# Matmul widths chosen on the chip by an expert's token count, and rows turned between its two products

## The chip, the cores and the metric

The kernel runs on one core of a Trainium2 chip. A core has five engines with instruction streams of their own: TensorE (PE, matrix products and transposes), VectorE (DVE), ScalarE (ACT), GpSimd (POOL) and SyncE (SP, which here only issues DMAs). Each engine's sequencer takes the instructions in order and hands them to the engine. The metric is the device time of one execution in microseconds; the time of a version is the median over its runs.

## The reference

Two stages. The first is attention over a short window with some global positions, for 4 batches of 768 positions and 8 heads of 64 numbers. Its result, 3072 rows (tokens) of 512 numbers, is the input of the second, a mixture of eight experts, of which each token uses one:

```python
xn = x / (norm(x) + 1e-6);  en = expert_emb / (norm(expert_emb) + 1e-6)
logits = xn @ en.T / tau
expert_idx = argmax(logits, axis=1)
gate_w = softmax(logits)[arange(N), expert_idx]
for e in range(8):
    mask = expert_idx == e
    h = maximum(x[mask] @ w1[e], 0)          # 512 -> 1024
    out[mask] = gate_w[mask, None] * (h @ w2[e])   # 1024 -> 512
```

All numbers are float32. How many tokens an expert gets is known only while the kernel runs.

## The kernel before, in words

The attention stage (`window_attention`) writes the 3072 rows to `x_dram` and routes them: for each token it finds the expert, its rank among the expert's tokens and its gate, and scatters the pair (token number, gate) to a slot of the table `meta`. Expert e owns the slots from e*3072 on, filled in order of rank; unused slots hold token number 3072 (a row of zeros in `x_dram`, and out of bounds for `out`) and gate 0. The tile `cnt` holds the tokens counted for each expert.

The expert stage is a loop over eight experts with a fixed capacity of 512 slots (`CAP`), that is four tiles of 128. The function `load_rows` loads the slots (`emt`), makes the token numbers whole numbers (`ids`, line 636) and gathers the rows by four indirect DMAs (`xg`, line 640). The function `expert` then does, in this order:

- 16 transposes on PE (line 655), four to a bank of PSUM, each bank copied by DVE into `xT` (line 656), which has the 512 slots along its free dimension;
- the first product: eight blocks of 128 hidden numbers, two to a tile `big` (two banks), each block over four pieces of 128 inputs, always 512 slots wide (line 664); ACT applies the Relu to both blocks at once (line 666). In float32 the profile shows two matmul instructions for each `matmul` of the code, so a first product has 64;
- the second product: for each of the four tiles of slots, eight pieces of hidden numbers into one bank `work` (line 671); DVE scales by the gate into `y` (line 674) and POOL scatters the rows to `out` (line 675). Again 64 matmul instructions.

Four `work` banks and two `big` tiles fill the eight banks of PSUM. The weights of an expert, 2 MB each for `w1` and `w2`, lie in one of two buffers, and SP loads the next ones when the buffer comes free. A scheduler sets the order of all engines' instructions and the semaphores between them.

After the last expert, `leftover` handles what the fast path can't: experts with more than 512 tokens. A flag is loaded into a register of every engine (line 699), and a branch (line 700) skips the pass when nothing is left.

Of the kernel before, what the change touches and what calls it, by code (L numbers as in the profile page):

```python
# [9 lines left out]
F32 = mybir.dt.float32  # L10
I32 = mybir.dt.int32
AF = mybir.ActivationFunctionType
ALU = mybir.AluOpType
AX = mybir.AxisListType
PSUM = bass.MemoryType.PSUM

P = 128
NEG = 1e9
CAP = 512

# [47 lines left out]
def empty_slots(k):  # L70

    k.nc.sync.dma_start(k.meta[:].rearrange("(p c) w -> p c w", p=P), k.fill[:])
# [57 lines left out]
def load_weights(k, e, w):  # L130
    nc = k.nc
    nc.sync.dma_start(w[0][:], k.w1[e].rearrange("(c p) f -> p c f", p=P))
    nc.sync.dma_start(w[1][:], k.w2[e].rearrange("(f p) m -> p f m", p=P))


def new_weights(k, pool):
    w1 = pool.tile([P, k.NC, k.F], F32, name="w1t", tag="w1t")
    w2 = pool.tile([P, k.NF, k.DM], F32, name="w2t", tag="w2t")
    return w1, w2
# [137 lines left out]
def window_attention(k, ctx):  # L277
    nc, tc, NT, D, B, S, H, E = k.nc, k.tc, k.NT, k.D, k.B, k.S, k.H, k.E

    def pool(name, bufs, **kw):  # L280
        return ctx.enter_context(tc.tile_pool(name=name, bufs=bufs, **kw))

    sp_p, od_p, tp_p = (pool("wa_sp", 1, space=PSUM), pool("wa_od", 4, space=PSUM),
                        pool("wa_tp", 2, space=PSUM))
    const = pool("wa_const", 1)
# [340 lines left out]
def load_rows(k, slots):  # L626

    nc, NJ = k.nc, CAP // P
    mt = k.gp.tile([P, NJ, 2], F32, name="emt", tag="emt")
    i = nc.sync.dma_start(mt[:], slots.rearrange("(p j) w -> p j w", p=P))  # L630
    for sc in k.scatters or []:
        k.tc.add_manual_dep(i.ins, sc.name,
                            mybir.DependencyInfo(mybir.DependencyClass.Sync, mybir.DependencyReason.DATA),
                            reason="a slot comes from any of the scatters")
    ids = k.gp.tile([P, NJ], I32, name="ids", tag="ids")
    nc.vector.tensor_copy(out=ids[:], in_=mt[:, :, 0])
    xgs = []
    for j in range(NJ):
        xg = k.xgp.tile([P, k.DM], F32, name="xg", tag="xg")
        nc.gpsimd.indirect_dma_start(  # L640
            out=xg[:], out_offset=None, in_=k.x_dram[:],
            in_offset=bass.IndirectOffsetOnAxis(ap=ids[:, j : j + 1], axis=0),
        )
        xgs.append(xg)
    return mt, ids, xgs


def expert(k, rows, w1, w2):
    nc, NJ = k.nc, CAP // P
    mt, ids, xgs = rows  # L650
    xT = k.xtp.tile([P, k.NC, CAP], F32, name="xT", tag="xT")
    for j in range(NJ):
        ps = k.work.tile([P, k.NC, P], F32, name="work", tag="work")
        for c in range(k.NC):
            nc.tensor.transpose(ps[:, c, :], xgs[j][:, c * P : (c + 1) * P], k.ident[:])  # L655
        nc.vector.tensor_copy(out=xT[:, :, j * P : (j + 1) * P], in_=ps[:])  # L656

    hT = k.hp.tile([P, k.NF, CAP], F32, name="hT", tag="hT")
    for f2 in range(k.NF // 2):
        ps = k.big.tile([P, 2, CAP], F32, name="big", tag="big")  # L660
        for i in range(2):
            f = 2 * f2 + i
            for c in range(k.NC):
                nc.tensor.matmul(ps[:, i, :], lhsT=w1[:, c, f * P : (f + 1) * P], rhs=xT[:, c, :],  # L664
                                 start=c == 0, stop=c == k.NC - 1)
        nc.scalar.activation(hT[:, 2 * f2 : 2 * f2 + 2, :], ps[:], AF.Relu)  # L666

    for j in range(NJ):
        ps = k.work.tile([P, k.DM], F32, name="work", tag="work")
        for f in range(k.NF):  # L670
            nc.tensor.matmul(ps[:], lhsT=hT[:, f, j * P : (j + 1) * P], rhs=w2[:, f, :],  # L671
                             start=f == 0, stop=f == k.NF - 1)
        y = k.yp.tile([P, k.DM], F32, name="y", tag="y")
        nc.vector.tensor_scalar_mul(y[:], ps[:], mt[:, j, 1:2])  # L674
        nc.gpsimd.indirect_dma_start(  # L675
            out=k.out[:, :], out_offset=bass.IndirectOffsetOnAxis(ap=ids[:, j : j + 1], axis=0),
            in_=y[:], in_offset=None, bounds_check=k.N - 1, oob_is_err=False,
        )


def leftover(k):


    nc, tc, E = k.nc, k.tc, k.E
    passes = -(-k.N // CAP)
    more = passes - 1
    flags = k.const.tile([P, 2], F32, name="flags")
    ps = k.work.tile([P, 512], F32, name="work", tag="work")
    nc.vector.tensor_tensor(out=k.good[:], in0=k.good[:], in1=k.fits[:], op=ALU.mult)
    nc.tensor.matmul(ps[:, 0:1], lhsT=k.ones[:], rhs=k.good[:], start=True, stop=True)  # L690
    nc.vector.tensor_scalar(out=flags[:, 0:1], in0=ps[:, 0:1], scalar1=float(P), scalar2=None,
                            op0=ALU.is_lt)
    most = k.const.tile([P, 1], F32, name="most")
    nc.vector.tensor_reduce(out=most[:], in_=k.cnt[:], op=ALU.max, axis=AX.X)
    nc.vector.tensor_scalar(out=flags[:, 1:2], in0=most[:], scalar1=float(CAP), scalar2=flags[:, 0:1],
                            op0=ALU.is_gt, op1=ALU.max)
    fi = k.const.tile([P, 2], I32, name="fi")
    nc.vector.tensor_copy(out=fi[:], in_=flags[:])
    any_ = nc.values_load(fi[0:1, 1:2], min_val=0, max_val=1)
    with tc.If(any_ > 0):  # L700
        redo = nc.values_load(fi[0:1, 0:1], min_val=0, max_val=1)
        with tc.If(redo > 0):
            nc.vector.memset(k.cnt[:], 0.0)
            k.scatters = None
            empty_slots(k)
            with ExitStack() as inner:
                dense_attention(k, inner)
        with ExitStack() as inner:
            expert_pools(k, inner)
            wp = inner.enter_context(tc.tile_pool(name="lo_w", bufs=1))  # L710
            rem = k.const.tile([P, E, passes], F32, name="rem")
            for j in range(passes):
                nc.vector.tensor_scalar(out=rem[:, :, j], in0=k.cnt[:], scalar1=-float(CAP * j), scalar2=0.0,
                                        op0=ALU.add, op1=ALU.max)
            nc.vector.tensor_scalar_mul(rem[:, :, 0], rem[:, :, 0], flags[:, 0:1])
            ci = k.const.tile([P, E * passes], I32, name="ci")
            nc.vector.tensor_copy(out=ci[:], in_=rem[:].rearrange("p e j -> p (e j)"))
            nc.sync.dma_start(k.c_dram[:, :], ci[0:1, :])
            with tc.For_i(0, E * passes, 1) as i:
                cv = k.gp.tile([1, 1], I32, name="cv", tag="cv")  # L720
                nc.sync.dma_start(cv[:], k.c_dram[:, bass.ds(i, 1)])
                n = nc.values_load(cv[0:1, 0:1], min_val=0, max_val=k.N)
                with tc.If(n > 0):
                    e, j = i // passes, i % passes
                    w1, w2 = new_weights(k, wp)
                    nc.sync.dma_start(w1[:], k.w1[bass.ds(e, 1)].rearrange("o (c p) f -> p (o c) f", p=P))
                    nc.sync.dma_start(w2[:], k.w2[bass.ds(e, 1)].rearrange("o (f p) m -> p (o f) m", p=P))
                    expert(k, load_rows(k, k.meta[bass.ds(e * k.N + j * CAP, CAP), :]), w1, w2)


def expert_pools(k, ctx):
# [8 lines left out]
def kernel(  # L740
# [13 lines left out]
    n = Net()  # L754
    n.tc, n.nc = tc, tc.nc
    nc = n.nc
# [19 lines left out]
    with ExitStack() as moe:  # L776
        wp_a = moe.enter_context(tc.tile_pool(name="wp_a", bufs=1))
        n.w = [new_weights(n, wp_a)]
        with ExitStack() as inner:
            window_attention(n, inner)  # L780

        n.work = ctx.enter_context(tc.tile_pool(name="work", bufs=4, space=PSUM))
        n.big = ctx.enter_context(tc.tile_pool(name="big", bufs=2, space=PSUM))
        wp_b = moe.enter_context(tc.tile_pool(name="wp_b", bufs=1))
        expert_pools(n, moe)
        for e in range(n.E):
            rows = load_rows(n, n.meta[e * n.N : e * n.N + CAP, :])
            if e > 0:
                w = new_weights(n, (wp_a, wp_b)[e % 2])
                load_weights(n, e, w)  # L790
            else:
                w = n.w[0]
            expert(n, rows, *w)
    n.scatters = None
    leftover(n)


# [26 lines left out]
```

## Time and profile before

| | |
|---|---|
| median of 3 runs | 772.12 us (770.15 to 774.82) |
| profiled execution, its own time | 777.63 us |
| its span, first to last instruction | 775.8 us |
| mean granted TensorE clock | 0.95 |
| attention, routing and first gather | until about 294 us of the span |
| eight experts | about 294 to 760 us |

In the profile, PE is TensorE's matmuls and PEld its weight loads, which run beside them. "PE big L664 x64" is a stretch of 64 matmuls of line 664 that write the tile `big`. An engine's name with a q behind it (PEldq, ACTq) is its sequencer: branches, register operations and semaphore waits that the engine itself never sees. The shape 128x512 behind a matmul is that of what streams through the array. The 40 digits of the page's slices are tenths; one slice is 19.4 us.

### The profile page before, as it was taken

The numbers are of one execution on the slowest core, as the hardware profiler recorded it, in microseconds if no ns is written. First come the engines' busy times: TensorE is split into PE (matmuls) and PEld (weight loads), VectorE is DVE, ScalarE is ACT, GpSimd is POOL, SyncE is SP. The second block draws the span as 40 slices with busy tenths as digits, with TensorE's granted clock in tenths as the row PEclk, the third lists the DMA queues.
The fourth block names the chain that finished last, engine by engine and source line by source line (L and its number), as shares of the span: only waits on it lengthen the run. The fifth ranks groups of instructions, "written<-read, shape, count | busy, mean of one in ns | idle before, by whom it ended". The sixth has DMA issues, their size and how long they took to land.

```text
span 775.8 us, 8382 instructions
## 1 busy us (share of the span) xinstructions
PE 686.5 (88%) x3394; PEld 353.0 (46%) x3394; DVE 182.4 (24%) x500; ACT 147.6 (19%) x280; POOL 112.6 (15%) x131
## 2 busy tenths in 40 slices
PE   4989986989799519999999999999999999999992
PEld 2556654555465304444444444444444444444440
DVE  2435562664366601011011011011011011011010
ACT  3545532543453200100100100100100100100100
POOL 2110022013003232012012012012012011010010
PEclk9999989898999758999999999999999999999996
DMA  9977669650110922214214115115114114000000
GB/s 185 213 129 213 177 177 39 137 118 7 37 42 16 283 48 90 83 58 174 81 53 171 78 71 175 71 64 172 64 70 168 64 77 146 0 37 14 0 26 18
DMA packets 99898, 74.57 MB, mean 96 GB/s; under 512 B 80762, under 2 KB 80890, under 8 KB 99850
## 3 DMA queue, kind: packets, MB, share of 16 engines
q1 hardware_dynamic: 90538, 58.44, 29.8%
q0 software_dynamic: 5888, 14.71, 5.4%
q10 hardware_dynamic: 3424, 0.79, 0.6%
q8 instruction: 29, 0.48, 0.3%
q14 instruction: 19, 0.16, 0.1%
HBM read 61.11 MB, written 14.90 MB: 98 GB/s over the span
## 4 chain that ended last, share of the span: by engine, by line
PE 59%; DVE 4%; DMA 3%; issue 0%; POOL 0%; SPq 0%; ACT 0%; DVEq 0%; ACTq 0%
PE big L664 29%; PE work L671 28%; DVE xT L656 2%; DMA x_dram<-xs 1%; DMA xg<-x_dram,ids 1%; DMA meta<-mt,slot 1%; DVE y L674 1%; PE tp L405 0%; PE tp L430 0%; PE tp L408 0%; DMA emt<-meta 0%; PE od L367 0%; PE work L655 0%; POOL out_dram L675 0%; SPq L630 0%
## 5 line engine op out<-in xcount | busy, mean ns | idle before, releaser
L664 PE MATMUL big<-xT,w1t 128*128 128x512 f32 x512 | 224.0, 598 | 11.2 <-DVE xT L656 11.2
L671 PE MATMUL work<-w2t,hT 128*128 128x512 f32 x512 | 221.0, 592 | 0.0
L664 PEld LDWEIGHTS big<-xT,w1t 128*128 128x128 f32 x512 | 97.4, 192 | 133.2 <-issue 120.0
L671 PEld LDWEIGHTS work<-w2t,hT 128*128 128x128 f32 x512 | 97.3, 190 | 122.5 <-issue 122.5
L674 DVE TENSOR_SCALAR y<-work,emt 128x512 f32<-128x512 f32 x32 | 24.0, 751 | 387.2 <-PE work L671 387.2
L666 ACT ACTIVATE hT<-big 128x1024 f32<-128x1024 f32 x32 | 32.8, 1023 | 432.0 <-PE big L664 432.0
L347 DVE TENSOR_TENSOR ex<-ex,table 126x384 f32<-126x384 f32 (+1 forms) x128 | 70.1, 585 | 89.0 <-ACT ex L341 89.0
L675 POOL DMA_INDIRECT out_dram<-y,ids x32 | 31.8, 995 | 337.8 <-DVE y L674 330.1
L337 PE MATMUL sp<-qT,kT 64*126 64x192 f32 (+1 forms) x512 | 66.8, 364 | 7.9 <-ACT qT L325 5.8
L367 PE MATMUL od<-ex,v 126*64 126x192 f32 (+1 forms) x576 | 62.6, 320 | 8.6 <-issue 4.6
L341 ACT ACTIVATE ex<-sp 126x768 f32<-126x768 f32 x64 | 49.1, 767 | 82.6 <-PE sp L337 60.8
L337 PEld LDWEIGHTS sp<-qT,kT 64*126 64x126 f32 x512 | 43.9, 196 | 28.1 <-issue 13.1
L367 PEld LDWEIGHTS od<-ex,v 126*64 126x64 f32 x576 | 34.1, 138 | 28.5 <-issue 18.6
L640 POOL DMA_INDIRECT xg<-x_dram,ids x32 | 30.9, 966 | 85.4 <-issue 42.9
L373 PE MATMUL od<-ex,ones 126*32 126x192 f32 (+1 forms) x576 | 36.3, 321 | 0.0
L655 PE MATMUL work<-ident,xg 128*128 128x128 f32 x128 | 17.7, 293 | 18.9 <-DMA xg<-x_dram,ids 18.9
L199 POOL DMA_INDIRECT meta<-mt,slot x24 | 23.8, 993 | 44.1 <-DVE slot L190 30.3
L655 PEld LDWEIGHTS work<-ident,xg 128*128 128x128 f32 x128 | 15.5, 151 | 23.7 <-DMA xg<-x_dram,ids 20.1
L320 PE MATMUL tp<-ident,k 128*128 128x128 f32 x96 | 19.7, 329 | 6.3 <-DMA k<-in_k_dram 6.0
L311 POOL COPY v<-v 30x1792 f32<-30x1792 f32 x8 | 13.6, 1698 | 74.8 <-DMA v<-in_v_dram 46.6
L430 PE MATMUL tp<-ident,xd 128*128 128x128 f32 x96 | 16.3, 298 | 8.2 <-DVE lh L420 6.3
L656 DVE COPY xT<-work 128x512 f32<-128x512 f32 x32 | 20.1, 682 | 6.8 <-PE work L655 6.5
(113 smaller groups left out, 297.4 us busy)
## 6 DMA issues: line engine op xcount, KB each, us to landing
w1t<-in_moe_w_dram SPq DMA_DIRECT2D x8, 2048.0 KB, 7.9
w2t<-in_moe_w_dram SPq DMA_DIRECT2D x8, 2048.0 KB, 10.8
k<-in_k_dram SPq DMA_DIRECT2D x32, 192.0 KB, 3.5
v<-in_v_dram SPq DMA_DIRECT2D x32, 192.0 KB, 4.5
x_dram<-xs SPq DMA_DIRECT2D x24, 256.0 KB, 6.3
q<-in_q_dram SPq DMA_DIRECT2D x28, 192.0 KB, 3.9
q<-in_q_dram ACTq DMA_DIRECT2D x4, 192.0 KB, 6.1
xg<-x_dram,ids POOLq DMA_INDIRECT x32
```

The source lines that it names most:

```text
L337: nc.tensor.matmul(sp[0:ROWS, e, a * n : (a + 1) * n], lhsT=t.kT[rows, j, 0:ROWS], rhs=t.qT[rows, j * BLK : j * BLK + n], start=True, stop ...
L341: nc.scalar.activation(ex, sp[0:ROWS, :, 0 : 2 * n], AF.Exp, scale=k.scale)
L347: nc.vector.tensor_tensor(out=exv, in0=exv, in1=tb, op=ALU.mult)
L367: nc.tensor.matmul(od[a][e * D : (e + 1) * D, cols], lhsT=g.v[0:ROWS, 2 * a + e, j, :], rhs=ex[:, e, a * n + c0 : a * n + c1], start=first ...
L373: nc.tensor.matmul(od[2][32 * i : 32 * i + 32, cols], lhsT=k.ones[0:ROWS, 0:32], rhs=ex[:, e, a * n + c0 : a * n + c1], start=first, stop= ...
L655: nc.tensor.transpose(ps[:, c, :], xgs[j][:, c * P : (c + 1) * P], k.ident[:])
L656: nc.vector.tensor_copy(out=xT[:, :, j * P : (j + 1) * P], in_=ps[:])
L664: nc.tensor.matmul(ps[:, i, :], lhsT=w1[:, c, f * P : (f + 1) * P], rhs=xT[:, c, :], start=c == 0, stop=c == k.NC - 1)
L666: nc.scalar.activation(hT[:, 2 * f2 : 2 * f2 + 2, :], ps[:], AF.Relu)
L671: nc.tensor.matmul(ps[:], lhsT=hT[:, f, j * P : (j + 1) * P], rhs=w2[:, f, :], start=f == 0, stop=f == k.NF - 1)
L674: nc.vector.tensor_scalar_mul(y[:], ps[:], mt[:, j, 1:2])
L675: nc.gpsimd.indirect_dma_start(out=k.out[:, :], out_offset=bass.IndirectOffsetOnAxis(ap=ids[:, j : j + 1], axis=0), in_=y[:], in_offset=No ...
```

## The change

The change does the following things.

- Slots are dealt to the tiles in order: tile j now holds the slots from 128 j on (`"(j p) w -> p j w"`), where slot 4 p + j had been in tile j. The filled slots so come first in `xT`.
- `choose_widths` compares the counts with thirteen widths, 128 and then 160 to 512 in steps of 32, on DVE, and loads two numbers for each expert into registers of PE: the index of the smallest width that holds all its tokens, and its number of tiles less one.
- The matmuls of the first product are written in thirteen versions, one for each width, for each of the four `big` tiles; those of the second in four versions, with one to four tiles. `tc.Switch` on PE picks the version (an "arm") by the register. Only PE takes part; the Relu still covers 512 columns, and all four tiles are still scaled and scattered, the unused ones to no row.
- The eight banks of PSUM are allocated once, cleared at the start, and taken in turn.
- PE's order is written out (`manual_schedule`): the rows of expert e+1 are turned between the first and the second product of expert e, and their slots and rows are fetched before expert e is computed.

```diff
+WIDTHS = [128] + list(range(160, CAP + 1, 32))
...
-    i = nc.sync.dma_start(mt[:], slots.rearrange("(p j) w -> p j w", p=P))
+    i = nc.sync.dma_start(mt[:], slots.rearrange("(j p) w -> p j w", p=P))
...
+def expert(k, rows, xT, w1, w2, choice=None, between=None):
+    nc, tc, NJ = k.nc, k.tc, CAP // P
+    mt, ids, _ = rows
+    def arms(i, n):
+        if choice is None:
+            return [n - 1]
+        return tc.Switch({PE: choice[i]}, n)
     hT = k.hp.tile([P, k.NF, CAP], F32, name="hT", tag="hT")
     for f2 in range(k.NF // 2):
-        ps = k.big.tile([P, 2, CAP], F32, name="big", tag="big")
-        for i in range(2):
-            f = 2 * f2 + i
-            for c in range(k.NC):
-                nc.tensor.matmul(ps[:, i, :], lhsT=w1[:, c, f * P : (f + 1) * P], rhs=xT[:, c, :],
-                                 start=c == 0, stop=c == k.NC - 1)
+        ps = banks(k)
+        for arm in arms(0, len(WIDTHS)):
+            w = WIDTHS[arm]
+            for i in range(2):
+                f = 2 * f2 + i
+                for c in range(k.NC):
+                    nc.tensor.matmul(ps[:, i, 0:w], lhsT=w1[:, c, f * P : (f + 1) * P], rhs=xT[:, c, 0:w],
+                                     start=c == 0, stop=c == k.NC - 1)
         nc.scalar.activation(hT[:, 2 * f2 : 2 * f2 + 2, :], ps[:], AF.Relu)
+    if between:
+        between()
+    ys = [bank(k) for _ in range(NJ)]
+    for arm in arms(1, NJ):
+        for j in range(arm + 1):
+            for f in range(k.NF):
+                nc.tensor.matmul(ys[j][:], lhsT=hT[:, f, j * P : (j + 1) * P], rhs=w2[:, f, :],
+                                 start=f == 0, stop=f == k.NF - 1)
     for j in range(NJ):
...
+def choose_widths(k):
+    nc, E, V = k.nc, k.E, len(WIDTHS)
+    over = k.const.tile([P, E, V], F32, name="over")
+    nc.vector.memset(over[:], 0.0)
+    for i, w in enumerate(WIDTHS[:-1]):
+        nc.vector.tensor_scalar(out=over[:, :, i], in0=k.cnt[:], scalar1=float(w), scalar2=None, op0=ALU.is_gt)
+    pick = k.const.tile([P, 2, E], F32, name="pick")
+    nc.vector.reduce_sum(out=pick[:, 0, :], in_=over[:], axis=AX.X)
...
+    k.choices = [[nc.values_load(pi[0:1, i, e : e + 1], engines=(PE,), min_val=0, max_val=(V, CAP // P)[i] - 1)
+                  for i in range(2)] for e in range(E)]
...
+        n.bigs = [ps.tile([P, 2, CAP], F32, name="big%d" % i) for i in range(2)]
+        n.works = [ps.tile([P, 512], F32, name="work%d" % i) for i in range(4)]
+        for t in n.bigs + n.works:
+            nc.vector.memset(t[:], 0.0)
+        choose_widths(n)
...
+        with tc.manual_schedule(engines={PE}):
+            prepare(0)
+            turn()
+            w = n.w[0]
+            for e in range(n.E):
+                now, next_ = next_, Net()
+                now.w = w
+                if e + 1 < n.E:
+                    prepare(e + 1)
+                    w = new_weights(n, (wp_a, wp_b)[(e + 1) % 2])
+                    load_weights(n, e + 1, w)
+                expert(n, now.rows, now.xT, *now.w, now.choice, turn if e + 1 < n.E else None)
```

Here `prepare(e)` takes the expert's two registers and calls `load_rows`, `turn` calls `turn_rows` (the 16 transposes with their four copies, as before), and `bank` and `banks` hand out the PSUM banks in turn.

## The prediction

> **What bounds the kernel now.** I read the page first (busy shares, then the chain that ended last), then the chain in order of time over the expert stage, then the single lines around one hand-over between experts.
>
> ```profile
> PE 686.5 (88%) x3394; PEld 353.0 (46%) x3394; DVE 182.4 (24%) x500; ACT 147.6 (19%) x280; POOL 112.6 (15%) x131
> q8 instruction: 29, 0.48, 0.3%
> L671 PE MATMUL work<-w2t,hT 128*128 128x512 f32 x512 | 221.0, 592 | 0.0
> ```
>
> PE is the bound, and the second product (L671) never waits before its matmuls (0.0). The q8 row will matter too: 29 packets carry 0.48 MB, about 16 KB each, while PE ran 6788 instructions: code arrives in blocks of some 240 instructions. In order of time, the chain shows one expert after another:
>
> ```profile
> 382.34 27.48 PE work L671 x64
> 409.82 0.02 issue
> 409.85 0.75 DVE y L674
> 410.60 2.40 DVE xT L656 x4
> 413.00 0.04 issue
> 413.05 27.73 PE big L664 x64
> 440.78 27.48 PE work L671 x64
> ```
>
> An expert costs 27.73 (first product) + 27.48 (second) + 3.2 us in which PE waits for the turned rows: 58.4 us, eight times from 294 to 760 us. A first product is 64 matmuls of 0.433 us, so each of its four pairs of hidden blocks takes 27.73/4 = 6.93 us; a tile of the second takes 27.48/4 = 6.87 us.
>
> Where PE's sequencer stands beside its array is read from the lines of L655 between 396 and 413 us and, for the one branch in the program, from those of L700:
>
> ```profile
> L655 PE MATMUL work<-ident,xg x16: 272/272/273, 409.6 to 411.3; 128*128 128x128 f32 x16
> L655 PEldq EVENT_SEMAPHORE  x4: 51/51/51, 401.9 to 407.1; - x4
> L700 ACTq COMPARE_BRANCH  x1: 50/50/50, 762.3 to 762.3; - x1
> L700 PEldq COMPARE_BRANCH  x1: 4402/4402/4402, 762.4 to 762.4; - x1
> L700 PEldq EVENT_SEMAPHORE  x2: 51/51/51, 766.8 to 767.0; - x2
> ```
>
> The sequencer waits for the transposes' rows at 401.9, while the array reaches those transposes at 409.6: it runs 7.7 us ahead, 36 instructions. And PE's only taken branch, over the leftover pass, held its sequencer for 4.40 us.
>
> **The change part by part.** Routing the reference's own inputs gives 406, 310, 510, 319, 322, 369, 472 and 364 tokens per expert. The chosen widths are 416, 320, 512, 320, 352, 384, 480, 384 (sum 3168 of 4096), the tiles 4, 3, 4, 3, 3, 3, 4, 3 (27 of 32).
>
> *Array work removed.* A 512-wide matmul takes 433 ns and its weight load 190 ns beside it; the narrowest chosen, 320, takes 271 ns by proportion, still above the load, so time goes with width. First products: (4096-3168)/512 x 27.73 = 50.3 us. Second: 5 tiles x 6.87 = 34.4 us. Together 84.6 us, all on the path.
>
> *Rows turned between the products.* The 16 transposes take 1.91 us and the four copies to xT 2.48 us (timeline at 409.6 and 410.5). They leave the hand-over, but the second product now needs the same four banks and waits for the last copy: 0.5 for the first four transposes + 2.5 = 3.0 us there, against 3.2 before. I take nothing for it. The Relu (1.02 us) lies under the transposes.
>
> *The switches.* Five jumps into an arm and five out, per expert. The thirteen arms of a first-product switch hold 13 x 32 instructions, more than one code block, and the chosen arm is the 7th to 13th; so I price a jump in like L700's, 4.4 us, not like ACT's 0.05. Ahead of it the sequencer works out the target: 0.5 us, an estimate from the 181 ns register operation of L699 and some at 50 ns. Issuing 32 instructions takes 1.9 us (16 transposes with their loads in 1.91 us: 60 ns each). The jump out lies between 0.05 and whatever is left of 4.4 us after the issue, 2.5 us; I take 0.3, nearer to the low end, since the code behind the switch is known on entry and can be on its way. One cycle of the sequencer is 0.5+4.4+1.9+0.3 = 7.1 us; the array needs 27.73/4 x 3168/4096 = 5.36 us on average. So the sequencer, not the array, sets the first product.
>
> The sequencer leaves the second product 7.7 us ahead; 0.3+0.5+4.4 later it is in the first arm, 2.5 us early. First product: -2.5 + 3 x 7.1 + 5.4 = 24.2 us (21.4 by the array alone). It entered the last arm at 18.8, leaves at 21.0, issues the transposes by 23.2, and is in the arm of the second product at 23.2+4.9 = 28.1, against turned rows at 24.2+3.0 = 27.2. The second product takes 27.48 x 27/32 = 23.2 us on average. An expert: 51.3 us instead of 58.4, eight times 7.1 = 57 us saved.
>
> [...]
>
> *Arms of unequal length.* An arm with three tiles signals once less than one with four; the missing signals must be made up, as the EVENT_SEMAPHOREs of L700 do behind the skipped block, and they can't go out before the tiles' own. So I let the sequencer wait there for the array: its lead of 7.7 us is lost. The next first arm is entered 5.2 us after the second product instead of 2.5 us before it. Four experts with three tiles have a successor: 4 x 7.7 = 31 us. The other end is 0, if no signal is missing.
>
> *At the start and the end.* The first expert's sequencer waits for gathered rows and only then jumps: 4.9 us where 1.9 us of waiting stood, +3. The slots' new layout lands four pieces of 8 bytes per partition instead of one of 32; the load took 2.1 us (281.79 to the cast at 283.90), between 0 and four times that, +1, on the first expert alone. The last four evictions and scatters may bunch, +1. Sum +5.
>
> *What costs nothing.* Some 17 small DVE operations choose the widths (0.17 us each, 3 us), DVE clears eight PSUM banks (some 5 us at the rate of the y evictions, 0.75 us for 512 columns), PE loads 16 registers (492 ns by L699: 7.9 us). All fit between the last routing operation at 272.2 and the first gathered rows at 288.3; without that cover up to 8 us. Weights (4 MB an expert, landing in 7.9 and 10.8 us), gathers and scatters (8 at 1.3 us on POOL) stay inside an expert of 46 us or more, and the next expert's gather is issued a whole expert early. ACT still reads 512 columns, 1.02 us beside PE.
>
> *Clock.* The first product of the first expert follows thin PE work; its window shows a granted clock of 0.93 and 29.8 us for 64 matmuls instead of 27.7: 2.1 us. Gaps of 2 to 5 us between arms could bring that once an expert, 0 to 17 us. I take 0, because the 3.2 us hand-over shows 1.00.
>
> *Sum.* Span 775.8 - 57 + 31 + 5 = 755; with 1.83 us around it (777.63 for the profiled run) 757. That run was 5.5 us above the median of 772.12, so 751 us.
>
> **The rivals.**
>
> *The jumps are free or hidden.* If arms lie in code already fetched, the cycle is 0.5+0.3+1.9+0.3 = 3.0 us, below any arm, and the lead hides it. Then 775.8 - 84.6 + 1 = 692, or 687 us as a median. For it: no sequential crossing of a code block shows as a stall in the chain. Against: L700.
>
> *The way out costs a fetch of its own; this ends slower.* If leaving an arm waits for another block, fetched from entry on in 4.4 us, the cycle becomes 0.5+4.4+4.4 = 9.3 us. The three further entries, and the entry into the second product, each come 2.2 us later: 8 x 4 x 2.2 = 70 us. Then 751 + 70 = 821; without the lost lead some 31 less, 790. The point is where a cycle exceeds 7.1 + 21/32 = 7.8 us: above that the change loses. For it: the same 4.4 us row, and an arm too short (1.9 us of issue) to cover it.
>
> *Every arm ends with the array drained.* If leaving the first product's arms also waits for the array, each of four arms costs 0.3+0.5+4.4 = 5.2 us on top of its 5.4: 42 us instead of 24.2 per expert, some +140 from the forecast at most, and less where waits overlap: 850 to 890 us. Nothing in the rows asks for it, since those arms signal alike.
>
> **How the numbers follow.** Forecast 0.40 (its own range 730 to 772, from no lost lead beside a dearer way out to a cycle of 7.8); free jumps 0.15; dear way out 0.38; drained arms 0.07. A measurement of this kernel tells 0.5%, 4 us, from no change. Faster: 0.15 and 0.36 of the forecast's 0.40; same: 0.06, from its upper edge and the dear case's lower one; slower 0.43. The range runs from 690, just above the free jumps, to 815: it leaves out the drained arms, the worst of the dear way out, and the lowest of the free case.
>
> **What would show it.** In the profile after: L664's successors at 271 ns for width 320 and in proportion; gaps on PE of 1.5 to 2 us between arms of sixteen matmuls, labelled issue rather than a wait for ACT; PE's sequencer in indirect branches of some 4 us, 40 of them; code packets on q8 up from 29 to well over 100; a gap of 5 us behind three-tile second products and none behind four-tile ones. No gaps between arms would prove the forecast wrong towards 690; gaps above 2.8 us on average, towards 815. Matmuls at 433 ns whatever the width would mean that no narrower arm was taken.

## The result, and the profile after

The changed kernel takes 827.59 us (median of 4 runs, 821.51 to 832.04) against 773.47 us of the kernel before: 1.0701 times as long, 95% interval 1.062 to 1.0783. The prediction said 751 us, a gain; the time lies above its range (690 to 815), on the side and near the price of its second rival (821 us). The profiled run has a span of 830.3 us, 54.5 us more than before.

The page of the changed kernel, beside the lines shown of before:

```profile
PE 644.5 (78%) x3314; PEld 352.8 (42%) x3314; DVE 184.7 (22%) x523; ACT 148.1 (18%) x280; POOL 112.9 (14%) x131
PEclk9989998989997568998899999898998988998895
q8 instruction: 173, 2.83, 1.9%
L694 PE MATMUL big<-xT,w1t 128*128 128x320 f32 (+5 forms) x512 | 208.1, 568 | 72.9 <-issue 69.6
L704 PE MATMUL work<-w2t,hT 128*128 128x512 f32 x432 | 193.5, 609 | 20.2 <-issue 10.7
```

The work did shrink: 432 instead of 512 matmuls in the second product, and narrower ones in the first. But PE is now idle before them, 72.9 us in the first product, and almost all of that is "issue": time in which the array waits for no semaphore that the profile shows. Code arrives in 173 packets instead of 29. The granted clock has 8s among its 9s all through the expert stage; before, it had only 9s there:

```profile
PEclk9999989898999758999999999999999999999996
```

The mean of that stage is 0.91 instead of 1.00.

Where the array waits for no semaphore, the sequencer is the place to look. These are the lines of PE's branch instructions over the whole run, then the branches and the prefetch hints inside one first product (expert 3, 320 wide, 493 to 528 us). The columns are count, shortest/median/longest in ns, and first and last start:

```profile
L894 PEldq COMPARE_BRANCH  x80: 320/4534/7626, 297.1 to 796.1; - x80
```

```profile
L894 PEldq COMPARE_BRANCH  x8: 3352/4492/5162, 492.5 to 527.9; - x8
L689 PEldq BRANCH_PREFETCH_HINT  x3: 36/41/45, 501.4 to 520.7; - x3
```

Forty switches make 80 branches, in and out, and the median branch holds the sequencer for 4.5 us. In the first product both of a switch do: the hint, the first instruction of an arm, stands at 501.4 and two arms later at 520.7, so one arm takes the sequencer 9.65 us. The 16 matmuls of an arm follow each other every 0.27 us where the clock is full, 4.3 us in all; so they do in two of these four arms. In the other two most come at half that pace, and the arms take 6.1 and 7.2 us, still less than 9.65.

That such a jump waits for code can be read from the code queue. These are its lines for the stretches of three jumps: 521.0 (4.60 us), 527.9 (3.45 us) and 673.3 (7.63 us):

```profile
q8 instruction: 2, 0.03, 4.7%
q8 instruction: 1, 0.02, 1.6%
q8 instruction: 2, 0.03, 2.8%
```

So it is throughout this trace: in each of the 53 jumps of 4 to 6 us, and in the two above, two 16 KB packets of code start; in each of the sixteen of 2.7 to 3.9 us, one; in the eight under 0.5 us, and in one of 1.94 us that was hinted 1.3 us ahead, none. A jump with packets ends 1.3 to 2.3 us after the last of them. The waits of PE in the expert stage fit this:

```profile
PE big L694 <- issue: 69.6, 21, 5.4
PE work L704 <- issue: 10.7, 2, 5.9
PE work L704 <- DVE xT L671: 9.5, 6, 2.1
PE big L694 <- ACT hT L696: 3.3, 2, 1.8
```

Relu and row copies hold PE for 13 us together, issue for 80. The 54.5 us split by the starts of matmuls in the two traces:

| | before | after | difference |
|---|---|---|---|
| start of the span to the first matmul of expert 0 | 294.06 | 300.81 | +6.8 |
| from there to the last matmul of expert 7 | 465.8 | 502.6 | +36.8 |
| from there to the end of the span | 16.0 | 26.9 | +10.9 |

The last row is a cost of its own, seen in the timeline of the end:

```profile
804.04 2.73 DVE L708 TENSOR_SCALAR y<-work,emt 128x512 f32<-128x512 f32 x4 [58.71 <-PE work L704]
805.07 0.98 POOL L709 DMA_INDIRECT out_dram<-y,ids  x1 [48.27 <-DVE y L708]
808.57 0.98 POOL L709 DMA_INDIRECT out_dram<-y,ids  x1 [2.52 <-DVE fi L752]
813.35 0.98 POOL L709 DMA_INDIRECT out_dram<-y,ids  x1 [3.80 <-DMA out_dram<-y,ids]
816.75 0.98 POOL L709 DMA_INDIRECT out_dram<-y,ids  x1 [2.42 <-DMA out_dram<-y,ids]
```

The tile's eviction is DVE's line 708, the scatter POOL's line 709. Before, a tile was evicted and scattered while the next was multiplied. Behind a switch, DVE waits for the whole arm; then four evictions come at once, and the scatters follow 3.4 to 4.8 us apart; the brackets of the last two name the landing of the one before. Inside the stage this is beside PE's work; after the last expert it is on the path.

### The profile page after: what moved, and what is told of

The parts are those of the page before. It is cut to its first block, busy times and chain, and to the rows that moved or that the text cites. A ratio compares the mean times of both kernels' runs of the same rounds, so it can differ in the third digit from the quotient of the medians.

```text
span 830.3 us, 8699 instructions
## 1 busy us (share of the span) xinstructions
PE 644.5 (78%) x3314; PEld 352.8 (42%) x3314; DVE 184.7 (22%) x523; ACT 148.1 (18%) x280; POOL 112.9 (14%) x131
## 5 line engine op out<-in xcount | busy, mean ns | idle before, releaser
L694 PE MATMUL big<-xT,w1t 128*128 128x320 f32 (+5 forms) x512 | 208.1, 568 | 72.9 <-issue 69.6
L704 PE MATMUL work<-w2t,hT 128*128 128x512 f32 x432 | 193.5, 609 | 20.2 <-issue 10.7
L694 PEld LDWEIGHTS big<-xT,w1t 128*128 128x128 f32 x512 | 110.4, 220 | 170.5 <-issue 143.3
L704 PEld LDWEIGHTS work<-w2t,hT 128*128 128x128 f32 x432 | 83.7, 195 | 125.6 <-issue 114.7
L708 DVE TENSOR_SCALAR y<-work,emt 128x512 f32<-128x512 f32 x32 | 21.8, 744 | 171.7 <-PE work L704 171.7
L322 PE MATMUL tp<-ident,k 128*128 128x128 f32 x96 | 20.4, 339 | 5.9 <-DMA k<-in_k_dram 5.6
L322 PE MATMUL tp<-ident,q 128*128 128x128 f32 x96 | 20.4, 331 | 2.0 <-DMA q<-in_q_dram 1.1
```

What stands on the lines that cost most here:

```text
L322: nc.tensor.transpose(ps[:, r * P : (r + 1) * P], src[:, 3 * half + r, :, :], k.ident[:])
L694: nc.tensor.matmul(ps[:, i, 0:w], lhsT=w1[:, c, f * P : (f + 1) * P], rhs=xT[:, c, 0:w], start=c == 0, stop=c == k.NC - 1)
L704: nc.tensor.matmul(ys[j][:], lhsT=hT[:, f, j * P : (j + 1) * P], rhs=w2[:, f, :], start=f == 0, stop=f == k.NF - 1)
```

## The experiments

The theories. A: two fetches of code for each switch pace PE's sequencer at nearly 10 us an arm, longer than an arm's array work. B: the new order or the switch as a unit makes PE wait for other engines. C: narrower matmuls are not faster in proportion. D: the gaps let the granted clock fall, and the half-speed matmuls are the loss. The kernels below ran on different chips, on which the kernel before took 774 to 780 us, so ratios to it are compared.

**No choice on the chip: the arms written in.**

```diff
-        choose_widths(n)
+        n.choices = [[min(i for i, w in enumerate(WIDTHS) if w >= c), -(-c // P) - 1] for c in COUNTS]
...
+        if isinstance(choice[i], int):
+            return [choice[i]]
         return tc.Switch({PE: choice[i]}, n)
```

> The changed kernel with the arms picked while the program is written, from the counts of these inputs: same widths, tiles and order, no choice on the chip, no jump. Theory A (two fetches of code for each switch hold PE's sequencer for some 9.7 us an arm, longer than the arm): all of the loss is in the jumps, so an expert takes 21.4 (first product) + 3.0 (turned rows) + 23.2 (second) = 47.6 us and the span about 298 + 378 + 16 = 692, the median about 690 us. Rival B (the new order makes PE wait for Relu, banks or copies): 8 x 3 us or more on top, 715 us or above. Rival C (a narrower matmul isn't faster in proportion): first products as before, 740 us.

Measured: 692.81 us, ratio 0.8864 (0.8789 to 0.8939). Same widths, tiles and order without a jump; the page has 0.8 us of idle time before the first product's matmuls and none before the second's, and code packets are back to 28:

```profile
q8 instruction: 28, 0.46, 0.3%
L707 PE MATMUL work<-w2t,hT 128*128 128x512 f32 x432 | 186.7, 592 | 0.0
L697 PE MATMUL big<-xT,w1t 128*128 128x320 f32 (+5 forms) x512 | 174.2, 502 | 0.8 <-issue 0.8
```

C falls, and so does B for the new order: the whole loss, and the whole gain that it hides, hang on how the arms are reached. The switch as a unit is gone here together with the jumps, so this run doesn't test that half of B.

**The new order alone, 512 wide and four tiles.**

```diff
-        choose_widths(n)
+        n.choices = [[len(WIDTHS) - 1, CAP // P - 1] for _ in range(n.E)]
```

> The changed kernel with all arms fixed at 512 slots and four tiles while the program is written: the new order, the cleared banks and the new layout of slots alone. A: the hand-over of 3.2 us is replaced by one of 3.0 us between the products, and the start is 4 us later (the banks are cleared on DVE ahead of the last routing operations): 772 to 778 us. B: the order itself costs: 795 us or more.

Measured: 771.3 us, ratio 0.9867 (0.9797 to 0.9936), better than either theory said. The expert stage takes 454.1 us instead of 465.8, 1.7 us for each of seven hand-overs. The timeline between two products shows where:

```profile
387.60 1.91 PE L670 MATMUL work<-ident,xg 128*128 128x128 f32 x16
388.24 1.89 DVE L671 COPY xT<-work 128x512 f32<-128x512 f32 x3 [18.84 <-PE work L670]
389.35 1.02 PE L706 MATMUL work<-w2t,hT 128*128 128x512 f32 x2
```

Without a switch the second product needs only its own first bank, whose copy is done early, so it follows the transposes at once. Between this kernel and the one with the arms written in lie 454.1 - 370.1 = 84.0 us of expert stage: the prediction's 84.6 us of array work, nearly to the digit.

**Only the second product chooses; only the first does.**

```diff
 second only:
+        n.choices = [[len(WIDTHS) - 1, c[1]] for c in n.choices]
 first only:
+        n.choices = [[c[0], CAP // P - 1] for c in n.choices]
```

> Only the second product chooses on the chip; the first is fixed at 512. A: the one jump in an expert starts while the array is 7 us behind and is over by the time the turned rows are there, and the jump out is under a long arm (0.33 us in the trace): an expert takes 27.7 + 3.0 + 23.2 = 53.9 us, with the later start and the end of the changed kernel (26 us instead of 15, four scatters one after another) a span of about 755 to 760, a median of 752 to 757 us. If every switch costs its two fetches wherever it stands (9 us, eight times, less the 3 us it would wait anyway): 800 us.

> Only the first product chooses on the chip; the second is fixed at four tiles. A: the first product keeps its pace of 9.7 us an arm, the second takes 27.5 us: 34 us more array work than in the changed kernel, less some 12 us of waiting for the jump into the second product and less the bunched scatters at the end (11 us): 830 to 845 us, the slowest of the four. If the losses are spread evenly over the 40 switches (1.4 us each of the 55 us), this kernel would lose only 32 of them: near 820 us or below.

Measured: second only 762.17 us, ratio 0.9735 (0.966 to 0.9809); first only 844.84 us, ratio 1.0772 (1.0679 to 1.0865). Scaled to the 772 us the expectations were made against, that is 752 and 832 us, what A expects, at the lower edge both times. A jump out of a second product, hinted 13 us or more ahead, takes 0.3 us, and behind a second product of three tiles the next expert's matmuls follow after one pair's time, 0.43 us, as behind one of four. The net loss is in the 32 short arms of the first product. But the second product's switch isn't free. It removes 34.4 us of array work from the kernel with the new order alone, and that kernel's expert stage shortens by only 21.9 (454.1 to 432.2), while the end takes 26.3 us, 18.2 with the arms written in: some 20 us, which we put to the switch as a unit, theory B's other half, since it waits for all four banks and evicts late. The first-only kernel's agreement with A is in part chance: five of its jumps took 7.4 to 7.9 us, which the fill below explains.

**Half the jumps in the first product.** Each arm fills both `big` tiles, with two Relus behind it.

```diff
-    for f2 in range(k.NF // 2):
-        ps = banks(k)
+    for f4 in range(k.NF // 4):
+        pair = [banks(k) for _ in range(2)]
         for arm in arms(0, len(WIDTHS)):
             w = WIDTHS[arm]
-            for i in range(2):
-                f = 2 * f2 + i
+            for i in range(4):
+                f = 4 * f4 + i
```

> The changed kernel with two switches in a first product instead of four; each arm fills both big tiles, so that an arm takes 10.7 us on average, and the next waits for the Relu of both (2 us). A: the arm now covers the sequencer's 9.7 us; an expert takes 21.4 + 2 (Relu) + 3.0 (turned rows) + 1.3 (jump into the second product) + 23.2 = 51 us, a span of 735 us, 0.94 to 0.96 of the kernel before. If each switch costs the same share of the loss, 16 of 40 fewer give 22 us back: 1.04.

Measured: 741.8 us, ratio 0.9567 (0.9521 to 0.9612), as A has it. Sixteen switches fewer bring not 22 us but 11 points of the ratio, some 88 us. The line of the branches, then the largest wait of PE in the expert stage (20.4 us, where the changed kernel had 69.6):

```profile
L896 PEldq COMPARE_BRANCH  x48: 301/3684/7075, 293.6 to 709.5; - x48
PE big L694 <- issue: 20.4, 5, 5.1
```

A jump in kept its price (median 4.6 us, as in the changed kernel, both without those in front of a second product). A jump out didn't: the hint of a longer arm stands 4.9 to 8.6 us ahead of its exit, and eleven of the sixteen exits took under 1.7 us. So the longer arm helps twice, by more array work over the sequencer's cycle and by an earlier hint; this run doesn't part the two.

**Two widths instead of thirteen.**

```diff
-WIDTHS = [128] + list(range(160, CAP + 1, 32))
+WIDTHS = [384, 512]
```

> The changed kernel with two widths, 384 and 512, instead of thirteen (two arms, and two for the second product, three or four tiles); five experts run 384 wide, three 512. 16 us more array work in the first products, which a pace set by the sequencer hides. If every jump waits for its own block of code, near or far: within 15 us of the changed kernel, 1.05 to 1.08 of the kernel before. If only a far arm has to be fetched, as code that follows in sequence is there already: 0.93 to 0.96.

Measured: 808.51 us, ratio 1.0433 (1.0387 to 1.048), between the two expectations, nearer to that of every jump fetching. The branch line shows a smaller median:

```profile
L891 PEldq COMPARE_BRANCH  x80: 315/3572/7639, 291.0 to 777.9; - x80
```

In the trace, jumps into the arm that follows the switch took mostly 2.7 to 3.2 us, where the far arms of the changed kernel took 4.4 to 4.9; leaving that same arm, over the other one, took 4.5 to 5.1, while leaving the last arm, whose end comes next, took mostly 2.6 to 3.4. The 35 jumps of 2 to 4 us in this trace have one packet of code each. So near code saves one of two packets and about 1.5 us of a jump, not the jump. The ratio understates this, for seven jumps took 6.3 to 7.6 us here, for a reason that the next run shows.

**The gaps filled with matmuls of no use.**

```diff
         nc.scalar.activation(hT[:, 2 * f2 : 2 * f2 + 2, :], ps[:], AF.Relu)
+        if choice is not None and f2 < k.NF // 2 - 1:
+            for c in range(FILL):      # 4: eight matmul instructions
+                nc.tensor.matmul(k.works[0][:], lhsT=w1[:, c % k.NC, 0:P], rhs=xT[:, c % k.NC, :],
+                                 start=True, stop=True)
```

> The changed kernel with eight matmul instructions (512 wide, 3.5 us) of no use behind each of the first three arms of a first product, into a work bank that is overwritten later: PE's gaps are filled, the jumps are as before. A: the sequencer's pace of 9.7 us stays, the fill lies in the gaps for the narrow arms and adds a few us for the two widest: within 15 us of the changed kernel, on either side. Rival D (the gaps let the granted clock fall, 96 us of the expert stage at half speed, and that is the loss): the clock returns to 0.94 or more and the time falls by 30 to 48 us.

Measured: 857.76 us, ratio 1.109 (1.1022 to 1.1158). This speaks against D, for the clock rose (mean 0.924 instead of 0.893) and the time did too; but A's "within 15 us" fails as well. The branches tell why:

```profile
L899 PEldq COMPARE_BRANCH  x80: 316/4674/8115, 294.0 to 823.1; - x80
```

Nine jumps took over 6 us, against two in the changed kernel, and each began within 4 us of the start of a weight load: for one, SP issues `w2` at 500.0 and the jump at 502.8 takes 7.8 us. The edit had also changed the order of SP's loads. In the changed kernel `w1` and `w2` mostly start together at the end of a first product; here each `w2` starts at the end of a second product, into the jumps that follow. In eight of the nine the first code packet starts 1.9 to 4.1 us after the jump; the median of the changed kernel's jumps of 4 to 6 us is 0.4. Nine jumps at some 2.4 us over the median are 22 us; the changed kernel's two are 5, so up to 17 of the 30 us between the two kernels are explained. The same loads meet jumps in other runs: five over 6 us in the first-only kernel, seven with two widths, three with half the jumps. The next pair leaves the loads out.

**No weight loads in the way, without and with the fill.** All experts use the weights of the first two.

```diff
-                    w = new_weights(n, (wp_a, wp_b)[(e + 1) % 2])
-                    load_weights(n, e + 1, w)
+                    if e == 0:
+                        n.w.append(new_weights(n, wp_b))
+                        load_weights(n, 1, n.w[1])
+                    w = n.w[(e + 1) % 2]
```

> The changed kernel without the weight loads from the third expert on (the experts in the two buffers are used over and over, so the products are those of other weights): what do weight loads do to the jumps? If code is fetched at its own latency: jumps still 4 us or more and the time within 20 us of the changed kernel, the jumps of 6 us and above gone, 1.04 to 1.07. If jumps are slow because code queues behind weights throughout: jumps of 2.5 us or less, 0.97 or below.

> The kernel without later weight loads (products as there) and with the fill of eight matmul instructions behind the first three arms. It tells the clock from the jumps without the weights in the way. A: within 10 us of the kernel without the fill. D (the clock is the loss): 30 us or more faster than that one.

Measured: 827.19 us, ratio 1.0641 (1.0575 to 1.0708), and with the fill 833.97 us, ratio 1.0673 (1.0574 to 1.0772). The branches without later weight loads:

```profile
L896 PEldq COMPARE_BRANCH  x80: 324/4440/5389, 297.8 to 788.3; - x80
```

No jump is above 5.4 us, so the long ones were fetches behind weights; the median is nearly unchanged, so the others were not. The expert stage is 493.7 us instead of 502.6 in these two traces, and the ratios differ by 0.006 within their intervals: the loads cost the changed kernel some 5 to 9 us. And with the fill the time stays, although less of the stage runs at half clock (the windows over the expert stage, first without, then with the fill; the columns are the window, its length, the busy times with counts, PEclk, DMA share and GB/s):

```profile
301.89:795.54 493.65, 408.97 (x1055) 205.16 (x1056) 37.24 (x61) 32.78 (x32) 49.06 (x51) 0.92 0.11 29
```

```profile
304.22:807.04 502.82, 466.91 (x1248) 229.33 (x1248) 37.31 (x61) 32.79 (x32) 49.05 (x50) 0.98 0.10 28
```

0.92 to 0.98 in clock, and nothing gained. The fill is 87 us of array work itself, so the time alone is a weak test of D. The sequencer's rows are the stronger one: from one arm's entry to the next it takes 9.8 us on average without the fill and 10.0 with it, 9.9 in the changed kernel, of which 9.0 are the two jumps. So within a first product D falls: matmuls at half speed lie inside a cycle that the sequencer sets.

**One switch for an expert, and the banks cleared by ACT.** PE, ACT, DVE and POOL enter an arm that holds both products, the turned rows, evictions and scatters.

```diff
+    for arm in tc.Switch({e: now.choice for e in IN_ARM}, len(WIDTHS)):   # PE, ACT, DVE, POOL
+        w = WIDTHS[arm]
+        for f2 in range(k.NF // 2):
+            ps = k.bigs[f2 % 2]
...                                         # matmuls w wide; Relu
+        for j, xg in enumerate(nxt.rows[2]):
...                                         # next expert's rows turned, copied
+        for j in range(-(-w // P)):
...                                         # second product, y, scatter of tile j
 and, for the second kernel:
-            nc.vector.memset(t[:], 0.0)
+            nc.scalar.copy(out=t[:], in_=...)   # a tile of zeros
```

> One switch for an expert instead of five: PE, ACT, DVE and POOL all enter the arm, which holds both products, the turned rows between them, the evictions and the scatters, written for each of the thirteen widths. A (two fetches of code a switch, harmless under a long arm): the one jump in starts 7 us before the array runs dry and takes 5, the way out is fetched during the arm, so PE stays busy and the time comes close to the kernel with the arms written in (0.886 of the kernel before): 0.89 to 0.92. If a switch costs its 9 us wherever it stands, or if four engines that jump hold each other up: 8 x 9 us more, 0.98 or above.

> The kernel with one switch for an expert, with the eight banks cleared by ACT from a tile of zeros instead of by DVE. If the clearing on DVE, ahead of the last routing operations, is what makes the start of the expert stage later (the last slots are ready 3.2 us later in the changed kernel): 3 to 4 us less, 0.880 of the kernel before. If it was hidden: no change, 0.885.

Measured: 685.82 us, ratio 0.8849 (0.881 to 0.8888); with ACT clearing 686.44 us, ratio 0.8844 (0.8781 to 0.8907). The first beats both kernels, by a little more than A expected, and its expert stage, 370.0 us, is that of the kernel with the arms written in (370.1): the choice costs nothing there. PE's jumps and its only wait on that stage:

```profile
L926 PEldq COMPARE_BRANCH  x16: 311/2329/4887, 291.6 to 658.8; - x16
```

```profile
PE big L731 <- issue: 3.6, 1, 3.6
```

Eight jumps in still take 4.2 to 4.9 us each; they start while the array has matmuls queued, and only the first, with nothing queued ahead of it, is seen. The eight jumps out take 0.3 to 0.4 us. The last scatters are spread again. Clearing the banks on ACT cut the time from the last choice of experts to the slots from 6.9 to 3.4 us in the traces, but the medians don't show these 3.5 us: inconclusive within their interval.

## Why the prediction was wrong

*Array work removed, 84.6 us:* right (84.0 between the kernels without switches).

*The bound:* right. It said that PE's sequencer, not the array, would set the first product, and named the point: a cycle above 7.8 us loses. The first rival, free jumps, gave 687 us as a median (its own terms give 688), and that is about what the kernels without exposed jumps take: 686 us, and 693 on a chip on which the kernel before took 780.

*The step that failed is the price of the jump out,* "I take 0.3, nearer to the low end, since the code behind the switch is known on entry and can be on its way". The hint may send for it: a packet of code starts 0.6 to 1.4 us behind each of the 32 hints of the first product. But from the hint to the end of the exit it took mostly 4.7 to 5.3 us, and the sequencer reaches the exit 0.2 to 0.35 us after the entry. That is the second mis-sized term: issuing 32 instructions was priced at 1.9 us from the pace of 16 transposes, which is the array's pace; handing them over takes 0.2 to 0.35 us here. So even the upper end given, 2.5 us, was too low, and the cycle is 0.35 (target, by two MOVEs and a register operation) + 4.6 + 0.2 + 4.5, in the trace mostly 9.6 to 10.6 us for the arms up to 480 wide and 9.9 on average, instead of 7.1. Counted as the prediction counts it, from the first matmul of a first product to the first of the second, an expert takes 38.9 us on average instead of 28.1: 86 us over eight experts, more than the 57 us that the stage was to gain. (The prediction's 28.1 has a slip of 0.3 us: 21.0 + 1.9 is 22.9, not 23.2.)

*The jump in, 4.4 us from one row of L700:* right. The 32 jumps into arms of the first product took 4.65 us as a median, and two packets of code start inside 31 of them. PE's shortest branch at these switches took 320 ns, while the same switches cost the engines that take no part in them 32 to 53 ns a branch.

*Lead lost behind arms of three tiles, 31 us:* did not happen; 0.43 us behind three tiles and four alike. This error hid a third of the other one. That the measured time lies so near the second rival's 821 us is therefore partly luck: that sum still holds the 31 us, and without them it was 790.

*Rows turned between the products, nothing taken:* right for the switched kernel (3.0 us of hand-over in the kernel where only the second product switches), wrong for one without a switch, where 1.7 us an expert are gained. The switch waits as a unit for all four banks.

*Start, +4 forecast, +6.8 measured:* the jump was in it (2.2 us measured) and the slots' layout (0.6); the clearing of the banks, called free, was not (3.6). DVE did it between the last routing operations and so moved them, which the cover that was named, the wait for the gathers, could not hide.

*End, +1 forecast, +10.9 measured:* evictions held until the arm's end, and scatters 3.4 to 4.8 us apart. Of the 10.9, 2.2 are there without a switch too (18.2 us of end with the arms written in).

*Clock, nothing taken, 0 to 17:* the clock did fall (86 us of the expert stage at half speed in the trace), and the sequencer's cycle did not change when the fill raised it again. It cost something where PE was not waiting for its sequencer: three second products, behind gaps of 2.4 to 6.2 us, began at half speed, and the eight took 192.2 us instead of the forecast's 185.6.

Put right, 755 - 31 + 86 + 7 + 3 + 10 = 830 us of span: without the lost lead, with the dearer first products (the two jumps behind weight loads and the matmuls at half clock in them are inside the 86), the slower second products, the start and the end. 830.3 were measured. The 86, 7, 3 and 10 are read from the trace, so the sum shows that nothing large is missing, not that each part's cause is proved.

## What to carry to other kernels

A branch's price is paid by whoever its sequencer feeds, so set it against what the array still has queued when the sequencer reaches it: here some 7 us of lead hid a 4.6 us jump behind a long arm entirely, while an arm of 4 to 7 us could not cover the 9 us of its two jumps. A choice on the chip belongs where one arm holds tens of microseconds of work, with every engine that shares buffers inside the arm, so that waits, evictions and signals stay as fine as without it: with such arms, 46 us long on average, the expert stage took 370.0 us, against 370.1 with the arms written in. When a cost has ends far apart and the verdict turns on it, look for what the sequencer does between the two events, not for the kinder end.

## What the runs showed of the hardware that was not expected

- The time of a jump of PE went with the packets of code that started inside it: in the changed kernel two 16 KB packets in all 53 jumps of 4 to 6 us, one in all sixteen of 2.7 to 3.9 us, none in the eight of 0.3 to 0.45 us.
- A prefetch hint 0.2 to 0.35 us ahead of its branch brings nothing: such exits of the first product's arms took mostly 4.4 to 5.0 us where the end was not the next code in sequence, like unhinted jumps in. A hint 13 us or more ahead leaves 0.3 to 0.45 us. In between, at 4.9 to 8.6 us (the kernel with half the jumps), eleven of sixteen exits took under 1.7 us and five 3.7 to 5.0 us. A weight load started between hint and exit in three of these five, but also in three of the eleven; why those five were slow is open.
- PE's sequencer went from an arm's entry to its exit, past 32 instructions, in 0.17 to 0.35 us (1.2 to 1.7 us in the first arm from the second expert on, while the second product ahead of it still ran), while the array needed 4 to 7 us for them. Past 64 instructions, in the kernel with half the jumps, it took 4.9 to 8.6 us.
- Jumps of PE close behind the start of a weight load took up to 8.1 us instead of 4.5; without the later loads none took more than 5.4, and 5.6 with the fill.
